# Two plain groups in place of one at the start of each Strassen mixer

## The chip, the cores and the metric

The kernel runs on one core of a Trainium2 chip (trn2). The metric is the device time of one execution in microseconds. Before the change the median of three runs is 1559.9 us (1555.95 to 1565.29). The engines are named as in the profile: PE is TensorE's matmul, PEld its weight load, DVE is VectorE, ACT ScalarE, POOL GpSimd, and SP the SyncE, whose queue issues nearly all DMAs.

## What is computed

Attention with RMS-normalised q and k, and then two mixers over its output. All of it is in float32, for 4 batches of 448 tokens with 768 channels.

```python
def _moe_ref(x, U, V, w_ch1, w_ch2):          # mixer a: w_ch1 is 768 x 3072, w_ch2 3072 x 768
    h = x.transpose(0, 2, 1) @ U @ V
    u = x + h.transpose(0, 2, 1)
    return u + np.maximum(u @ w_ch1, 0.0) @ w_ch2

def _moe2_ref(x, w_tok1, w_tok2, w_ch1, w_ch2):   # mixer b: w_ch1 is 768 x 1536, w_ch2 1536 x 768
    h = np.maximum(x.transpose(0, 2, 1) @ w_tok1, 0.0) @ w_tok2
    u = x + h.transpose(0, 2, 1)
    return u + np.maximum(u @ w_ch1, 0.0) @ w_ch2
...
x = attn_out.transpose(0, 2, 1, 3).reshape(4, 448, 768)
return _moe2_ref(_moe_ref(x))
```

## The kernel before

**Numbers.** Every matmul operand is a pair of float32r tiles, a high part (ScalarE copies and rounds it) and a low part (what is left, by VectorE or GpSimd). A product takes three matmuls for each block of 128 channels: high x high, low x high, high x low. The helper `mm` (L79) records every one, so all of TensorE's rows show line 79 and are told apart by tile: ps_g is a plain first layer, ps_p a Strassen product, ps_x the second layer, ps_u and ps_t the token mixing ahead of a mixer, ps_o a transpose of the output.

**Order of the work.** The four batches go in two pairs. Attention of all batches runs beside the first pair's mixers a and b (`ffn`). Then the second pair goes through mixer a and mixer b, both in `pair_ffn`; this is the Strassen part, from about 1006 us to the end. The program is written as one stream and a list scheduler fixes the order on each engine at build time; an engine works its own list strictly in order and waits on semaphores. DMAs of chunks, copies and stores all stand on SP's queue, in order too.

**A mixer in `pair_ffn`.** The hidden columns are cut into chunks of 128, and G = 2 chunks make a group: 24 chunks or 12 groups in mixer a, 12 chunks or 6 groups in mixer b. The first and the last group are plain: for each batch `plain` makes 18 matmuls a chunk (6 channel blocks x 3) into a PSUM bank, `relu` splits the result into gs, and `second` adds gs x w2 onto the batch's own tile (xs, the tile xT) in six steps of 6 matmuls, each ended by a VectorE add (L664). The groups between take both batches at once with Strassen's method (`seven`): the two batches are its two columns, the group's two chunks its two rows, and the channels are cut in halves. Seven products of 9 matmuls replace the plain first layer's 72.

**What the products read.** On the weights' side `w1_blocks` loads the group's two w1 chunks (tiles w_a, tag "raw", two buffers), builds the sums s1 to s4 on VectorE (L223 to L226) and splits seven blocks, the low parts on GpSimd (L145). On the activations' side the sums t1 to t4 of the two batches' u are needed; they are made once a mixer. Since `second` overwrites u in place, the sums must be taken from u before that. In the kernel before, `keep_first` (L571) copies the first batch's u by two DMAs (L576) into the low halves of t3 and t4 before its `second` runs, and `sums` (L580) reads the second batch's u in place, in three steps of four subtractions (L592 to L596) and four splits (L587 on ScalarE, L588 on VectorE). All twelve splits stand in program order ahead of the second batch's `second` and of the first Strassen group.

```python
        drain(second(xs[0], [plain(us[0], ws) for ws in w1s], w2s))
        g1 = [plain(us[1], ws) for ws in w1s]
        b = sums(kept)
        ...
        rest_ = second(xs[1], g1, w2s)
        for j0 in range(G, n - G, G):
            ...
            for _ in seven(a, b, gs):
                next(rest_, None)
                next(rest_, None)
```

`rest_` is the second layer that is still open; two of its steps are written after each product, and the scheduler mixes them. For the first Strassen group it is the second batch's six steps, for all later ones the twelve steps of the group before.

**Buffers.** The weight chunks w (high and low) have four buffers each, so two groups' chunks do not fit at once beside a group in use: a chunk's load, issued by SP straight into the low buffer, waits until the matmuls that read the buffer's last content are through. PSUM banks: three for kind "m", two each for "s" and "p". The pool act has two buffers of the tag xT; the second pair holds one of them, and t1 takes the other.

Of the kernel before, what the change touches and what calls it, by code (L numbers as in the profile page):

```python
# [10 lines left out]
F32R = mybir.dt.float32r  # L11
U32 = mybir.dt.uint32
I64 = mybir.dt.int64
AF = mybir.ActivationFunctionType
# [10 lines left out]
def attention_then_two_mixers(  # L25
# [49 lines left out]
    def f(x):  # L75
        return x.bitcast(F32)
# [132 lines left out]
    def tmp():  # L209
        return pools["pu"].tile([P, S], F32, tag="pu", name="pu")  # L210
# [354 lines left out]
    def pair_ffn(nm, w1, w2, xs, us, a, after, half=None, last=lambda: None):  # L565
# [5 lines left out]
        def keep_first():  # L571

            ts = [pools["tb"].tile([P, 2, HC, S], F32R, tag=f"t{i}", name=f"t{i}")
                  for i in (2, 3, 4)]
            for h, t in enumerate(ts[1:]):
                nc.sync.dma_start(f(t[:, 1]), xs[0][:, h * HC:(h + 1) * HC])  # L576
            return ts

        def sums(kept):


            ts = [act.tile([P, 2, HC, S], F32R, tag="xT", name="t1")] + kept
            k3, k4 = kept[1:]
            x = xs[1]

            def part(t, c, v_):
                nc.scalar.activation(t[:, 0, c], v_, AF.Copy)  # L587
                nc.vector.tensor_sub(t[:, 1, c], v_, f(t[:, 0, c]))  # L588

            for c in range(HC):  # L590
                t1, t2, t3 = [tmp() for _ in range(3)]
                nc.vector.tensor_sub(t1, x[:, c], f(k3[:, 1, c]))  # L592
                nc.vector.tensor_sub(t2, x[:, HC + c], t1)
                nc.vector.tensor_sub(t3, x[:, HC + c], x[:, c])
                t4 = tmp()
                nc.vector.tensor_sub(t4, f(k4[:, 1, c]), t2)  # L596
                for t, v_ in zip(ts, (t1, t2, t3, t4)):
                    part(t, c, v_)
            return {f"t{i + 1}": (t[:, 0], t[:, 1]) for i, t in enumerate(ts)}
# [80 lines left out]

        w1s, w2s = chunks(0)
        kept = keep_first()
        drain(second(xs[0], [plain(us[0], ws) for ws in w1s], w2s))
        g1 = [plain(us[1], ws) for ws in w1s]
        b = sums(kept)
        b.update(b11=(uh[:, :HC], ul[:, :HC]), b21=(uh[:, HC:], ul[:, HC:]),
                 b22=(vh[:, HC:], vl[:, HC:]))
        rest_ = second(xs[1], g1, w2s)
        for j0 in range(G, n - G, G):
# [128 lines left out]
    def last():  # L818
        pools["split_u"] = nc.vector
        blocks.append(w1_blocks("a", G))  # L820
# [7 lines left out]
    pair_ffn("a", wa1, wa2, xs, us, blocks[0], mix, last=lambda: blocks.append(w1_blocks("b", G)))  # L828
# [33 lines left out]
```

## Time and profile before

| | |
|---|---|
| median of three runs | 1559.9 us |
| the profiled execution | 1559.57 us, of it a span of 1556.9 us |
| mean granted clock of TensorE | 0.984 |
| busy in the span: PE, PEld | 1465.8 us (94%), 1295.5 us (83%) |
| busy in the span: DVE, POOL, ACT | 1101.6 (71%), 813.9 (52%), 708.8 us (46%) |
| ps_x matmuls | 2592 |
| ps_g matmuls | 1584 |

The profile lists instructions with line, engine, the tiles written and read, and the idle time of the engine ahead of them with what ended it. Matmuls overlap, so the busy time of a matmul (some 370 ns) is longer than the time from one start to the next; lost time on TensorE is read from starts.

### The profile page before, as it was taken

The page shows a single profiled execution, that of the slowest core. Times are in us where ns is not written, and L with a number is a line of the kernel's source. Part 1 is how long each engine was busy: PE and PEld are TensorE (multiplying, and loading weights), DVE is VectorE, ACT ScalarE, POOL GpSimd, SP SyncE. Part 2 cuts the span into 40 slices and gives each one's busy share as a digit, 9 for nine tenths or more (in the row PEclk, how much of TensorE's full clock was granted, in tenths as well). Part 3 has the DMA queues.
Part 4 walks back from the last instruction along what each step waited for, and adds up shares of the span by engine and source line. Part 5 has one row for each costly group of instructions (what it writes and reads, how often), then busy time and mean ns, then how long its engine had stood idle before and what let it go on. Part 6 is the DMA issues. An engine that isn't in the chain of part 4 may idle for free.

```text
span 1556.9 us, 21606 instructions
## 1 busy us (share of the span) xinstructions
PE 1465.8 (94%) x7522; PEld 1295.5 (83%) x7522; DVE 1101.6 (71%) x1800; ACT 708.8 (46%) x1413; POOL 813.9 (52%) x844
## 2 busy tenths in 40 slices
PE   4998878999999999999899999899999999999998
PEld 3766667788888999888798998789999999988997
DVE  5897777887888888566958676596666665576753
ACT  4776755566666665343634443342322322342311
POOL 6988867777786665444735553042443523113420
PEclk9999978999999999999999999999999999999999
DMA  6566553656655444442515530411212111101202
GB/s 171 143 158 168 143 177 108 189 164 187 189 175 151 142 149 134 165 154 81 180 49 187 184 132 28 156 61 52 71 52 71 44 50 60 66 21 51 72 21 92
DMA packets 96588, 180.94 MB, mean 116 GB/s; under 512 B 8992, under 2 KB 66304, under 8 KB 96480
## 3 DMA queue, kind: packets, MB, share of 16 engines
q1 hardware_dynamic: 96160, 179.57, 37.7%
q8 instruction: 59, 0.97, 0.3%
q14 instruction: 49, 0.40, 0.1%
q10 hardware_dynamic: 320, 0.00, 0.0%
HBM read 107.19 MB, written 36.57 MB: 92 GB/s over the span
## 4 chain that ended last, share of the span: by engine, by line
PE 65%; DVE 11%; DMA 7%; POOL 6%; ACT 5%; issue 4%; SPq 1%; ACTq 0%; POOLq 0%; DVEq 0%
PE ps_x L79 26%; PE ps_g L79 14%; PE ps_p L79 10%; PE pv L79 3%; PE sc L79 3%; PE pt L360 2%; POOL w_bits L134 2%; PE ps_u L79 2%; DMA c_a<-w_bits 2%; PE ps_t L79 2%; DVE w_bits L126 2%; POOL w L145 1%; DMA ks<-both 1%; DVE w_bits L131 1%; DMA qs<-both 1%
## 5 line engine op out<-in xcount | busy, mean ns | idle before, releaser
L79 PE MATMUL ps_x<-gs,w 128*128 128x448 f32 x2592 | 577.7, 371 | 14.7 <-DVE xT L664 4.2
L79 PEld LDWEIGHTS ps_x<-gs,w 128*128 128x128 f32 x2592 | 485.0, 190 | 60.1 <-DVE xT L534 7.8
L79 PE MATMUL ps_g<-u,w 128*128 128x448 f32 x1584 | 343.9, 370 | 0.5 <-POOL u L443 0.3
L79 PEld LDWEIGHTS ps_g<-u,w 128*128 128x128 f32 x1584 | 296.1, 189 | 25.3 <-POOL u L443 0.7
L145 POOL TENSOR_TENSOR w<-w 128x768 fp32r<-128x768 f32 x44 | 87.0, 1984 | 223.8 <-ACT w L144 142.4
L134 POOL TENSOR_TENSOR w_bits<-w_bits,w_round 128x768 uint32<-128x768 uint32 (+3 forms) x80 | 144.0, 1799 | 105.7 <-DVE w_bits L131 41.7
L145 POOL TENSOR_TENSOR w<-w_bits,w 128x768 fp32r<-128x768 f32 (+3 forms) x82 | 148.3, 1816 | 75.9 <-ACT w L144 72.2
L664 DVE TENSOR_TENSOR xT<-ps_x,xT 128x448 f32<-128x448 f32 x216 | 128.4, 618 | 63.5 <-PE ps_x L79 62.3
L534 DVE TENSOR_TENSOR xT<-ps_x,xT 128x448 f32<-128x448 f32 x216 | 132.4, 618 | 41.0 <-PE ps_x L79 38.2
L341 POOL TENSOR_SCALAR p<-p,sm 112x448 f32<-112x448 f32 x192 | 133.8, 709 | 19.9 <-DVE sm L338 17.2
L334 ACT ACTIVATE p<-sc,nm 112x448 f32<-112x448 f32 x192 | 121.1, 634 | 49.6 <-DVE nm L332 46.9
L79 PE MATMUL sc<-ks,qs 128*112 128x448 f32 x384 | 118.7, 402 | 18.8 <-ACT p L334 13.4
L145 POOL TENSOR_TENSOR w_a<-w_a 128x384 fp32r<-128x384 f32 (+1 forms) x28 | 42.9, 1533 | 178.7 <-DVE w_t L223 122.7
L332 DVE TENSOR_REDUCE nm<-sc 112x1 f32<-112x448 f32 x192 | 116.1, 615 | 19.9 <-PE sc L79 18.9
L360 PEld LDWEIGHTS pt<-ident,p 112*112 112x112 f32 x768 | 89.2, 133 | 36.4 <-issue 11.0
L360 PE MATMUL pt<-ident,p 112*112 112x112 f32 x768 | 111.5, 260 | 4.5 <-POOL p L341 3.4
L635 DVE TENSOR_TENSOR pu<-ps_p,pu 128x448 f32<-128x448 f32 x98 | 59.2, 620 | 71.0 <-PE ps_p L79 70.9
L126 DVE TENSOR_SCALAR w_bits<-w_bits 128x768 f32<-128x768 f32 (+3 forms) x80 | 75.5, 943 | 45.5 <-ACT w_bits L125 45.3
L371 ACT ACTIVATE ph<-pt 112x448 fp32r<-112x448 f32 (+1 forms) x168 | 88.2, 544 | 35.8 <-PE pt L360 35.1
L130 ACT ACTIVATE w_round<-w_raw 128x768 uint32<-128x768 uint32 (+3 forms) x80 | 69.7, 872 | 74.8 <-POOL w_bits L134 71.3
L375 DVE TENSOR_TENSOR pl<-pt,ph 112x448 fp32r<-112x448 f32 x144 | 87.3, 615 | 11.1 <-ACT ph L371 10.8
L125 ACT ACTIVATE w_bits<-w_raw 128x768 f32<-128x768 f32 (+3 forms) x80 | 69.9, 876 | 53.3 <-POOL w L145 36.5
(106 smaller groups left out, 2285.3 us busy)
## 6 DMA issues: line engine op xcount, KB each, us to landing
w_raw<-in_moe_w_ch_dram SPq DMA_DIRECT2D x72, 768.0 KB, 4.4
ks<-both SPq DMA_DIRECT2D x92, 224.0 KB, 3.7
c_a<-w_bits SPq DMA_DIRECT2D x48, 384.0 KB, 3.1
qs<-both SPq DMA_DIRECT2D x96, 112.0 KB, 3.1
w<-c_a SPq DMA_DIRECT2D x28, 384.0 KB, 3.7
c_b<-w_bits SPq DMA_DIRECT2D x24, 384.0 KB, 3.2
w_a<-c_a SPq DMA_DIRECT2D x20, 384.0 KB, 2.9
w<-c_b SPq DMA_DIRECT2D x16, 384.0 KB, 3.5
```

What stands on the lines that cost most here:

```text
L79: nc.tensor.matmul(o, lhsT=l, rhs=r, start=start, stop=stop)
L126: nc.vector.tensor_scalar_max(f(w), f(w), TINY)
L134: nc.gpsimd.tensor_tensor(w, w, r, op=ALU.add)
L145: nc.gpsimd.tensor_sub(lo, w, f(hi))
L332: nc.vector.tensor_reduce(nm, sc, axis=AX.X, op=ALU.max, negate=True)
L334: nc.scalar.activation(p, sc, AF.Exp, bias=nm, accum_out=sm[:, c % 2:c % 2 + 1])
L341: nc.gpsimd.tensor_scalar(x, x, sm[:, i:i + 1], 1.0, op0=ALU.mult, op1=ALU.mult)
L360: nc.tensor.transpose(pt[:, c * CP:(c + 1) * CP], pr[c][:, kc * CP:(kc + 1) * CP], ident[:CP, :CP],)
L371: nc.scalar.activation(ph, pt, AF.Copy)
L375: nc.vector.tensor_sub(pl, pt, f(ph))
L534: nc.vector.tensor_add(xT[:, dc], px, xT[:, dc])
L664: nc.vector.tensor_add(xT[:, dc], px, xT[:, dc])
```

## The change

Each mixer begins with two plain groups instead of one, so its Strassen loop starts a group later. Both batches' u are now kept by DMA copies (four a mixer, L577), the sums read the copies alone, and their twelve splits are a generator that is written step by step between the steps of two second layers. The second batch's part of the second plain group, first layer and second, becomes `rest_` of the first Strassen group. `w1_blocks` is called ahead of time for chunk 2G instead of G. The lines of `relu`, `plus` and `second` move up by seven (L664 becomes L657, L615 L608, L635 L628); L588 becomes L591.

```diff
-        def keep_first():
-
-            ts = [pools["tb"].tile([P, 2, HC, S], F32R, tag=f"t{i}", name=f"t{i}")
-                  for i in (2, 3, 4)]
-            for h, t in enumerate(ts[1:]):
-                nc.sync.dma_start(f(t[:, 1]), xs[0][:, h * HC:(h + 1) * HC])
+        def keep():
+
+            t1 = act.tile([P, 2, HC, S], F32R, tag="xT", name="t1")
+            ts = [t1] + [pools["tb"].tile([P, 2, HC, S], F32R, tag=f"t{i}", name=f"t{i}")
+                         for i in (2, 3, 4)]
+            for t, x, h in ((ts[2], 0, 0), (ts[3], 0, 1), (ts[1], 1, 0), (ts[0], 1, 1)):
+                nc.sync.dma_start(f(t[:, 1]), xs[x][:, h * HC:(h + 1) * HC])
             return ts
 
-        def sums(kept):
...
+        def sums(ts):
 
             for c in range(HC):
...
-                nc.vector.tensor_sub(t1, x[:, c], f(k3[:, 1, c]))
-                nc.vector.tensor_sub(t2, x[:, HC + c], t1)
-                nc.vector.tensor_sub(t3, x[:, HC + c], x[:, c])
-                t4 = tmp()
-                nc.vector.tensor_sub(t4, f(k4[:, 1, c]), t2)
+                y2, x2, x1, y1 = [f(t[:, 1, c]) for t in ts]
+                t1, t2, t3, t4 = [tmp() for _ in range(4)]
+                nc.vector.tensor_sub(t1, x2, x1)
+                nc.vector.tensor_sub(t2, y2, t1)
+                nc.vector.tensor_sub(t3, y2, x2)
+                nc.vector.tensor_sub(t4, y1, t2)
                 for t, v_ in zip(ts, (t1, t2, t3, t4)):
-                    part(t, c, v_)
+                    nc.scalar.activation(t[:, 0, c], v_, AF.Copy)
+                    nc.vector.tensor_sub(t[:, 1, c], v_, f(t[:, 0, c]))
+                    yield
...
-        w1s, w2s = chunks(0)
-        kept = keep_first()
-        drain(second(xs[0], [plain(us[0], ws) for ws in w1s], w2s))
-        g1 = [plain(us[1], ws) for ws in w1s]
-        b = sums(kept)
+        def plains(i, ws):
+            return second(xs[i], [plain(us[i], w) for w in ws[0]], ws[1])
+
+        ws = chunks(0)
+        ts = keep()
+        parts = sums(ts)
+        drain(plains(0, ws))
+        for _ in plains(1, ws):
+            next(parts)
+        ws = chunks(G)
+        for _ in plains(0, ws):
+            next(parts)
+        drain(parts)
+        b = {f"t{i + 1}": (t[:, 0], t[:, 1]) for i, t in enumerate(ts)}
...
-        rest_ = second(xs[1], g1, w2s)
-        for j0 in range(G, n - G, G):
+        rest_ = plains(1, ws)
+        for j0 in range(2 * G, n - G, G):
...
-        blocks.append(w1_blocks("a", G))
+        blocks.append(w1_blocks("a", 2 * G))
...
-    pair_ffn("a", wa1, wa2, xs, us, blocks[0], mix, last=lambda: blocks.append(w1_blocks("b", G)))
+    pair_ffn("a", wa1, wa2, xs, us, blocks[0], mix, last=lambda: blocks.append(w1_blocks("b", 2 * G)))
```

The scheduler's order changes from the first product with t2 on; ahead of that all engines' lists are the same but for the copies. Three places of it matter.

TensorE at the start of mixer a, in the changed program. Here t_11118 is t2 and t_11119 is t3, and w_s and w_a are the weight blocks of the first Strassen group. The 17 and 19 ps_g are the first layer of the first plain group for the second batch, the 18 and 18 that of the second plain group for the first batch.

```order
L79 MATMUL ps_p<-u,w_a 128x448 x9
L79 MATMUL ps_g<-u,w 128x448 x17
L79 MATMUL ps_x<-gs,w 128x448 x6
L79 MATMUL ps_g<-u,w 128x448 x19
L79 MATMUL ps_x<-gs,w 128x448 x30
L79 MATMUL ps_p<-t_11118,w_s 128x448 x5
L79 MATMUL ps_g<-u,w 128x448 x18
L79 MATMUL ps_x<-gs,w 128x448 x6
L79 MATMUL ps_g<-u,w 128x448 x18
L79 MATMUL ps_p<-t_11118,w_s 128x448
L79 MATMUL ps_x<-gs,w 128x448 x3
```

Before, the first two matmuls with t2 came 4 ps_x after the 19 ps_g. Now they come 30 later, and five of them stand ahead of the second plain group. In mixer b the order between the last ps_u and the first two matmuls with t2 is 4 ps_g, 9 ps_p and 14 ps_g.

TensorE at the change from the first to the second Strassen group of mixer a. First before: t_11119 is t4, the product whose end frees the tile w_a for the next group; u,w_s is the product with s4; the next group begins with u,w_a, and t_11117,w_s is its first matmul with t2.

```order
L79 MATMUL ps_p<-t_11119,w_a 128x448
L79 MATMUL ps_x<-gs,w 128x448 x2
L79 MATMUL ps_p<-u,w_s 128x448 x9
L79 MATMUL ps_x<-gs,w 128x448 x3
L79 MATMUL ps_p<-u,w_a 128x448 x2
L79 MATMUL ps_x<-gs,w 128x448 x15
L79 MATMUL ps_p<-t_11117,w_s 128x448
L79 MATMUL ps_x<-gs,w 128x448 x6
```

And the same place in the changed program, where t_11117 is t1, t_11120 is t4 and t_11118 is t2:

```order
L79 MATMUL ps_x<-gs,w 128x448 x24
L79 MATMUL ps_p<-u,w_s 128x448 x9
L79 MATMUL ps_p<-t_11117,w_s 128x448 x3
L79 MATMUL ps_x<-gs,w 128x448 x6
L79 MATMUL ps_p<-t_11117,w_s 128x448 x6
L79 MATMUL ps_p<-t_11120,w_a 128x448 x9
L79 MATMUL ps_x<-gs,w 128x448 x9
L79 MATMUL ps_p<-u,w_a 128x448 x2
L79 MATMUL ps_x<-gs,w 128x448 x15
L79 MATMUL ps_p<-t_11118,w_s 128x448
L79 MATMUL ps_x<-gs,w 128x448 x12
```

The product with s4 (u,w_s) has moved from behind the product with t4 to ahead of it. From the end of the t4 product to the ps_x that follows the first matmul with t2 there are 2 + 9 + 3 + 2 + 15 + 1 = 32 matmuls before, and 9 + 2 + 15 + 1 = 27 now. The same place in mixer b has 36 before and 27 now. The six ps_x in the middle of the t1 product are the last to read the second plain group's w2 chunks; 15 matmuls lie between them and the end of the t4 product.

VectorE at that place in mixer a, in the changed program. L628 is the addition of two products, L608 the low half of a relu, L223 to L226 form the next group's s1, s3, s2 and s4, and L657 adds a second layer's step onto xT and so frees its PSUM bank.

```order
L628 TENSOR_TENSOR pu<-ps_p,pu 128x448 x5
L608 SCALAR_TENSOR_TENSOR gs<-pu,gs 128x448 x3
L223 TENSOR_TENSOR w_t<-w_a 128x384
L224 TENSOR_TENSOR w_t<-w_a 128x384
L225 TENSOR_TENSOR w_t<-w_t,w_a 128x384
L226 TENSOR_TENSOR w_t<-w_a,w_t 128x384
L657 TENSOR_TENSOR xT<-ps_x,xT 128x448 x7
```

Before, two of the relu halves (L615 there) came ahead of L223 and the third between L225 and L226; now all three come ahead.

## Rows read from the trace of the kernel before

**Rows 1.** The page, part 1: busy time, share of the span, instructions.

```profile
PE 1465.8 (94%) x7522; PEld 1295.5 (83%) x7522; DVE 1101.6 (71%) x1800; ACT 708.8 (46%) x1413; POOL 813.9 (52%) x844
```

**Rows 2.** TensorE's timeline: start, length (us), instruction, count.

```profile
1086.69 2.59 PE L79 MATMUL ps_x<-gs,w 128*128 128x448 f32 x12
...
1089.12 1.99 PE L79 MATMUL ps_p<-t,w_a 128*128 128x448 f32 x9
```

**Rows 3.** TensorE's timeline, a later change of Strassen groups.

```profile
1075.67 0.44 PE L79 MATMUL ps_p<-t,w_s 128*128 128x448 f32 x1 [0.37 <-DVE xT L664]
```

**Rows 4.** Stretches: length, PE, PEld, DVE, ACT, POOL (count), PEclk, DMA, GB/s.

```profile
1024.91:1027.11 2.20, 0.99 (x4) 0.50 (x4) 2.20 (x5) 1.91 (x5) 0.00 (x0) 1.00 0.00 0
1036.12:1045.25 9.13, 6.92 (x33) 5.83 (x31) 8.92 (x11) 4.19 (x8) 6.98 (x6) 1.00 0.13 44
1392.96:1398.47 5.51, 4.46 (x18) 2.96 (x17) 5.51 (x12) 4.03 (x8) 1.52 (x1) 1.00 0.41 143
1411.24:1422.38 11.14, 7.72 (x37) 6.58 (x35) 9.72 (x11) 5.11 (x9) 8.86 (x6) 1.00 0.21 70
1422.38:1426.90 4.52, 4.51 (x15) 4.06 (x15) 2.17 (x4) 0.03 (x1) 3.02 (x3) 0.62 0.01 4
```

**Rows 5.** TensorE's timeline; in brackets idle time and its end.

```profile
1026.60 0.68 PE L79 MATMUL ps_p<-t,w_s 128*128 128x448 f32 x2 [1.21 <-ACT t L587]
...
1394.83 1.49 PE L79 MATMUL ps_x<-gs,w 128*128 128x448 f32 x6 [0.43 <-ACT gs L614]
...
1045.25 1.48 PE L79 MATMUL ps_x<-gs,w 128*128 128x448 f32 x6 [2.12 <-DVE xT L664]
...
1422.38 2.58 PE L79 MATMUL ps_x<-gs,w 128*128 128x448 f32 x6 [2.12 <-DVE xT L664]
```

**Rows 6.** Instructions on tile ps_p: count, shortest, median, longest (ns).

```profile
L79 PE MATMUL ps_p<-u,w_s x126: 362/365/370, 1036.5 to 1500.8; 128*128 128x448 f32 x126
```

**Rows 7.** Groups by line and shape, from 1006 us: count, busy us, mean ns, idle.

```profile
L664 DVE TENSOR_TENSOR xT<-ps_x,xT 128x448 f32<-128x448 f32 x216 | 128.4, 618 | 63.5 <-PE ps_x L79 62.3
```

**Rows 8.** Landing times of the copies, those of mixer a, then of mixer b.

```profile
DMA to landing us min/median/max: 6.0/7.0/8.1
...
DMA to landing us min/median/max: 3.3/3.7/4.1
```

**Rows 9.** Groups by line and shape from 1006 us, ScalarE.

```profile
L587 ACT ACTIVATE t<-pu 128x448 fp32r<-128x448 f32 x24 | 13.4, 575 | 14.5 <-DVE pu L592 7.2 <-DVE pu L596 4.1 <-DVE pu L593 1.9
```

**Rows 10.** TensorE's timeline, last ps_u ahead of mixer b.

```profile
1386.07 1.38 PE L79 MATMUL ps_u<-w,xs 128*128 128x448 f32 x6
```

**Rows 11.** SP's timeline: issues of w and w_a loads at the change of groups.

```profile
1030.68 0.93 SPq L194 DMA_DIRECT2D w<-c_a  x2
...
1036.32 0.32 SPq L217 DMA_DIRECT2D w_a<-c_a  x1
...
1408.84 0.93 SPq L194 DMA_DIRECT2D w<-c_b  x2
...
1411.47 0.32 SPq L217 DMA_DIRECT2D w_a<-c_b  x1
```

**Rows 12.** The page, part 6: DMA issues, size, median us to landing.

```profile
w<-c_a SPq DMA_DIRECT2D x28, 384.0 KB, 3.7
...
w_a<-c_a SPq DMA_DIRECT2D x20, 384.0 KB, 2.9
```

**Rows 13.** GpSimd's timeline in mixer b, the two w splits.

```profile
1412.97 4.04 POOL L145 TENSOR_TENSOR w<-w 128x768 fp32r<-128x768 f32 x2 [10.58 <-ACT w L144]
```

**Rows 14.** VectorE's timeline at the change of groups, mixer b.

```profile
1415.76 1.67 DVE L223 TENSOR_TENSOR w_t<-w_a 128x384 f32<-128x384 f32 x1
...
1417.82 1.36 DVE L225 TENSOR_TENSOR w_t<-w_t,w_a 128x384 f32<-128x384 f32 x1
...
1419.11 1.42 DVE L615 SCALAR_TENSOR_TENSOR gs<-pu,gs 128x448 fp32r<-128x448 f32 x1
...
1420.45 1.35 DVE L226 TENSOR_TENSOR w_t<-w_a,w_t 128x384 f32<-128x384 f32 x1
```

More of the change, by code (lines that the diff above doesn't have):

```diff
@@ L569, in pair_ffn @@
         (uh, ul), (vh, vl) = us
-        def keep_first():
-            ts = [pools["tb"].tile([P, 2, HC, S], F32R, tag=f"t{i}", name=f"t{i}")
-                  for i in (2, 3, 4)]
-            for h, t in enumerate(ts[1:]):
-                nc.sync.dma_start(f(t[:, 1]), xs[0][:, h * HC:(h + 1) * HC])
-            return ts
-        def sums(kept):
[L582 to L588, printed above, removed]
-            for c in range(HC):
-                t1, t2, t3 = [tmp() for _ in range(3)]
-                nc.vector.tensor_sub(t1, x[:, c], f(k3[:, 1, c]))
-                nc.vector.tensor_sub(t2, x[:, HC + c], t1)
-                nc.vector.tensor_sub(t3, x[:, HC + c], x[:, c])
-                t4 = tmp()
-                nc.vector.tensor_sub(t4, f(k4[:, 1, c]), t2)
+        def keep():
[4 more added lines that the diff above has]
+                nc.sync.dma_start(f(t[:, 1]), xs[x][:, h * HC:(h + 1) * HC])
+            return ts
+        def sums(ts):
+            for c in range(HC):
+                y2, x2, x1, y1 = [f(t[:, 1, c]) for t in ts]
[4 more added lines that the diff above has]
+                nc.vector.tensor_sub(t4, y1, t2)
                 for t, v_ in zip(ts, (t1, t2, t3, t4)):
-                    part(t, c, v_)
-            return {f"t{i + 1}": (t[:, 0], t[:, 1]) for i, t in enumerate(ts)}
+                    nc.scalar.activation(t[:, 0, c], v_, AF.Copy)
+                    nc.vector.tensor_sub(t[:, 1, c], v_, f(t[:, 0, c]))
+                    yield
         def plain(u, ws):
```

## The prediction, made before the changed kernel was run

> **What bounds the kernel now.** I read the page first, then TensorE's timeline, then equal stretches of it, and last the queues and engines that feed the places where it stands. The page shows TensorE busy in 94% of the span [rows 1]. That is a busy share and no rate, so I took the rate from a stretch without a wait: twelve matmuls of 448 columns that start at 1086.69 are followed by the next group at 1089.12 [rows 2]. That is 2.43 / 12 = 0.2025 us each, and this is the price of a matmul below. In the Strassen part (1006 us to the end) TensorE starts its matmuls at about this spacing nearly everywhere: the later groups lose 0.4 us or less in one place [rows 3]. So there the time is the number of matmuls times 0.2025, plus the few stretches in which TensorE stands. What other engines save costs or gains nothing unless it shortens such a stretch.
>
> **Where it stands.** Five stretches, all at the start of a mixer, hold nearly all of it [rows 4]. The counts there include one matmul that still runs at the left edge, so I take one off each (for the first, 4 less 1 gives 3). Length less count times 0.2025:
> - mixer a, first product with t2: 2.20 - 3 x 0.2025 = 1.59 us
> - mixer a, change from the first Strassen group to the second: 9.13 - 32 x 0.2025 = 2.65
> - mixer b, first product with t2: 5.51 - 17 x 0.2025 = 2.07
> - mixer b, the same change of groups: 11.14 - 36 x 0.2025 = 3.85
> - mixer b, right after it: 4.52 - 14 x 0.2025 = 1.68, and here the granted clock is 0.62, so much of it ran at the lower of the two levels (1.2 instead of 2.4 GHz), after the engine had stood twice within 3 us.
>
> The sum is 11.84 us. What ended these waits [rows 5]: the sums that make t2 (L587, and the relu that queues with them), and at the change of groups a VectorE add, L664, which frees the PSUM bank that the next ps_x needs. That add was not itself slow; it stood in VectorE's queue behind L223 to L226, the four operations that form the next group's weight blocks.
>
> **The change, part by part.**
>
> *Matmuls.* The row of the product with s4 counts 126, nine a product, so there are 14 Strassen groups [rows 6]. Two become plain. A Strassen group has 7 x 9 = 63 matmuls ahead of its second layer, a plain one 2 x 2 x 18 = 72; the second layer is the same. That is 2 x 9 = 18 matmuls more, 18 x 0.2025 = +3.65 us, all on the path.
>
> *Work that leaves the other engines.* 24 VectorE, 13 ScalarE and 8 GpSimd instructions fewer. TensorE's pace hides them wherever it doesn't stand, so I cost them at nothing; were that cover gone, VectorE's 24 at 0.618 us [rows 7] would be worth 15 us at the most.
>
> *The copies and the sums.* Two more copies a mixer (the halves of the second batch's u), on SP's queue ahead of the last stores and of all chunk loads of the second plain group. In mixer a the last one waits for the old xT tile's last transposes. From these TensorE has 9 + 17 + 6 + 19 = 51 matmuls (10.3 us) to the end of the first plain group's relus, where the sums come up, and the two copies made there today took 6.0 and 8.1 us [rows 8]; that fits. The sums have more matmuls to hide behind than today, but the new order puts five matmuls of s2 x t2 ahead of the second plain group on TensorE, which need two of the three column blocks of t2. After that relu stand, one behind the other, the relu's two halves, six VectorE operations and ScalarE's half of t2: 0.58 + 7 x 0.62 + 0.58 = 5.5 us [rows 7, 9], and up to 2 us more if a GpSimd split falls beside them. TensorE comes there after 33 matmuls, 6.7 us. I bound the loss by 0 and 1.6 (today's), and take 0.9. In mixer b the last ps_u matmuls start at 1386.07 [rows 10] and end at 1387.3. From there the chain is a VectorE add (0.62), the issue (0.46 [rows 11]), the copy (3.3 to 4.1, as in mixer b today [rows 8]), the sum (0.62) and ScalarE's half of t2 (0.58): 1392.9 to 1393.7. TensorE arrives after 4 + 9 + 14 = 27 matmuls, at 1392.8. That loses 0.1 to 0.9, and t2's lower half and the relus queued behind it some 0.7 more; I take 1.4 (bounds 0 and, with a landing of 8.1, 5.6). Together 2.3 where today 3.66 is lost: -1.4 us.
>
> *Chunks of the second plain group.* Their w slots come free only as the first plain group ends. The w1 loads then have 53 matmuls (10.7 us), the w2 loads, behind the last ps_x, 33 (6.7 us). A load takes 3.7 us to land [rows 12], ScalarE's half about 1.0 (0.58 for 448 columns, so an estimate for 768) and GpSimd's 2.0 [rows 13]: 6.7. So this is just met, and I cost it at nothing; half a microsecond a mixer would show first.
>
> *The change of groups.* This I expect to get longer. Its length is a chain: the fourth t product ends and frees the raw tile, SP issues the next w_a load, it lands 2.9 us later [rows 12], ScalarE, VectorE (L223 to L226) and GpSimd split it, and only then L664 frees the bank. From the end of that product to the ps_x it takes 9.13 us in mixer a and 11.14 in mixer b [rows 4]. The difference is when the two w loads ahead of it leave: 5.4 us before the product's end in mixer a (1030.68 against 1036.12), 2.4 in mixer b (1408.84 against 1411.24) [rows 11]. In mixer b their GpSimd halves run from 1412.97 for 4.04 us [rows 13], and VectorE's L223 takes 1.67 us, L615 1.42 and L226 1.35 [rows 14], where the same engine's L664 takes 0.62. In the changed program the two loads wait for slots that the second layer of the second plain group frees, 15 matmuls or 3.0 us before the end of the fourth product, in both mixers: nearly mixer b's case. On the other side the L615 that sat between L225 and L226 is gone from there (three such operations now come ahead of L223). I take 10.1 us, between the two, and 9.13 and 11.14 as bounds. And TensorE has less to do meanwhile: from the fourth product to the ps_x that needs the bank the new order has 9 + 2 + 15 + 1 = 27 matmuls, 5.47 us, in place of 32 and 36, because the product with s4 now comes before it. So it loses 10.1 - 5.47 = 4.6 us in each mixer, 9.3 in place of 6.5: +2.8 us.
>
> A rule of the Trainium skill bears on this. The rows show two-input VectorE operations on SBUF at twice their length while GpSimd is at work [rows 13, 14], while L664, with one input in PSUM, keeps its 0.62 [rows 7]. The skill (SBUF — State Buffer, section "Who interferes with whom") says that a VectorE instruction with two SBUF inputs and a GpSimd instruction that reads SBUF exclude each other, the first to issue keeping the port for its whole length. The trace agrees for L223 to L226; by that rule seven such operations in a row (three relu halves, four block sums) would stand behind GpSimd here, which is the second rival below.
>
> *Clock.* One spell at the lower level today (1.68 us). With waits of 4.6 us I expect one again, perhaps two; bounds 0 and 3.36. I take 1.68: no difference.
>
> *Sum.* +3.65 - 1.4 + 2.8 + 0 = +5.05, on the profiled execution's 1559.57 us: 1564.6 us. (That execution stands 0.3 us under the median of the three runs, 1559.9, which lie within 9.3 us.) About 0.5%, 7.8 us, is what a measurement can tell from no change, so this counts as no change.
>
> **The rivals.**
> 1. *The waits go.* Two plain groups give the loads and sums enough time, and the chain at the change of groups shrinks to its bare parts (2.9 landing, four block sums at 0.55, one add 0.62, about 6.2 us), so each mixer loses 0.7 there, nothing at t2, and no clock spell. 3.65 - 11.84 + 1.4 = -6.8: 1552.8 us. For it speaks that later groups lose next to nothing [rows 3]; against it that the new order takes five to nine matmuls out of the cover. Even all five stretches gone gives 8.2 us, hardly more than what can be told. Chance 0.17, a third of it faster by over 0.5%.
> 2. *GpSimd shuts VectorE out (the other side).* At the change of groups all seven two-input operations meet the w splits, the chain is mixer b's 11.14 or longer, both mixers lose 5.7 us or more, t2 in mixer a keeps its 1.6, and both get a spell at the lower clock: 3.65 + (1.6 + 1.4 - 3.66) + (11.4 - 6.5) + 1.68 = +9.6: 1569.2 us. It decides from a chain of about 10.8 us on. For it speaks mixer b's row; against it that the three relu halves could run before GpSimd starts. Chance 0.18.
> 3. *The copy of the second batch's u is late.* In mixer b it lands after 8.1 us, as the longest did in mixer a, instead of 3.3 to 4.1: 5.6 us lost at t2 in place of 1.4, so 1568.8 us. For it speaks that copies which leave together took twice as long [rows 8]; against it that in mixer b little else is moving then. Chance 0.08.
> 4. *The change does little of either:* the five stretches keep their length and only the matmuls count, 1563.2 us; this lies in the forecast's own range.
>
> **How the numbers follow.** The forecast (with case 4) has 0.57, rival 1 0.17, rival 2 0.18, rival 3 0.08. Faster by over 0.5%: a third of rival 1 and a little for a bound that I missed, 0.07. Slower by over 0.5%: nearly all of rival 2, most of rival 3 and a tenth of the forecast, 0.17 + 0.06 + 0.04 = 0.27. Within: 0.66. The range goes from 1555.5, short of rival 1, to 1572, past rival 2 with a late copy of 2 us.
>
> **What would show it.** In the changed profile: ps_g rows 144 more and ps_p rows 126 fewer, and 0.2025 us between matmuls as before. Up to 1017 us the two timelines should agree. At the change from first to second Strassen group, a wait of 4 to 5 us in each mixer that ends at the add into xT, with L223 to L226 above 1 us each and GpSimd at work beside them. If the four take 0.55 each, the first rival is right; if they and the relu halves all stretch, the second. At t2 a wait under 2 us in each mixer; one of 5 in mixer b that ends at a copy is the third. The prediction is wrong if a wait of over 3 us stands anywhere else, at the chunks of the second plain group above all.

## The result, and the profile after

The changed kernel took 1569.6 us (median of 17 runs, 1564.7 to 1576.2); the kernel before, run beside it, 1559.9 us (17 runs, 1555.5 to 1565.3). The ratio is **1.0055, with a 95% interval of 1.0041 to 1.0069**: slower by 8.6 us (6.4 to 10.8), where +4.7 was forecast against the same median. The two medians themselves lie 9.7 us apart; the ratio is used below. The time lies inside the range, at the value of the second rival (1569.2 us), and just past the half per cent that counted as no change.

First the page of the changed kernel, part 1, which answers to [rows 1], and a row of the view by tile (count, then shortest, median and longest in ns).

```profile
PE 1474.5 (94%) x7540; PEld 1296.5 (83%) x7540; DVE 1089.7 (70%) x1778; ACT 703.5 (45%) x1403; POOL 808.1 (52%) x836
```

```profile
L79 PE MATMUL ps_p<-u,w_s x108: 362/368/369, 1058.8 to 1510.3; 128*128 128x448 f32 x108
```

TensorE has 18 matmuls more (7540 against 7522), and the product with s4 went from 126 to 108 [rows 6]: two groups fewer, as counted. Next the stretches in which TensorE stands, cut at its matmul starts as in [rows 4]: length, then busy time and count of PE, PEld, DVE, ACT and POOL, granted clock, DMA share, GB/s. They are, for mixer a and then for mixer b: the first product with t2, the second plain group's chunks, the change from the first Strassen group to the second, and what follows it.

```profile
1021.30:1023.68 2.38, 1.06 (x4) 0.38 (x2) 2.38 (x5) 0.58 (x1) 0.17 (x1) 1.00 0.00 0
1032.76:1033.81 1.05, 0.37 (x2) 0.00 (x0) 0.41 (x1) 0.89 (x2) 0.00 (x0) 1.00 0.03 12
1067.76:1075.20 7.44, 4.13 (x17) 2.67 (x15) 7.40 (x9) 3.40 (x7) 5.29 (x5) 0.93 0.02 8
1075.20:1081.16 5.96, 5.95 (x16) 5.31 (x17) 2.79 (x5) 0.00 (x0) 4.00 (x4) 0.52 0.00 0
1401.03:1403.07 2.04, 1.97 (x8) 1.24 (x7) 2.04 (x5) 1.88 (x4) 0.00 (x0) 1.00 0.80 315
1407.73:1409.06 1.33, 0.77 (x4) 0.38 (x2) 1.33 (x3) 0.00 (x0) 1.33 (x2) 1.00 0.00 0
1451.32:1458.69 7.37, 3.94 (x17) 2.74 (x15) 7.34 (x9) 3.04 (x7) 5.75 (x5) 1.00 0.02 8
1458.69:1464.03 5.34, 5.33 (x18) 4.80 (x19) 2.79 (x5) 0.00 (x0) 4.01 (x4) 0.68 0.00 0
```

Each count holds one matmul that still runs over the left edge, except in the fourth and eighth row, ahead of which TensorE stood. Length less starts times 0.2025 us:

| lost, us | before | forecast | after |
|---|---|---|---|
| t2, mixers a + b | 1.59 + 2.07 | 2.3 | 1.77 + 0.62 = 2.39 |
| chunks of the second plain group | - | 0 | 0.85 + 0.72 = 1.57 |
| change of groups | 2.65 + 3.85 | 9.3 | 4.20 + 4.13 = 8.33 |
| lower clock after it | 0 + 1.68 | 1.68 | 2.72 + 1.69 = 4.41 |
| sum | 11.84 | 13.3 | 16.70 |

16.70 - 11.84 + 3.65 for 18 matmuls = +8.5 us, close to the 8.6 of the ratio. The two profiled executions differ by more: from the first start of a ps_p to the last of a ps_x it is 543.2 us before (1006.66 to 1549.89) and 554.4 after (1004.47 to 1558.87), 11.2 us. The 2.7 us that the table doesn't hold are matmuls that follow one another a little more slowly in some stretches, without a wait (last section).

Now the change of groups in mixer a, from the timeline (start, length, engine, line, operation, count; in brackets idle time and what ended it).

```profile
1063.71 1.99 PE L79 MATMUL ps_p<-t,w_a 128*128 128x448 f32 x9
...
1065.53 1.99 PE L79 MATMUL ps_x<-gs,w 128*128 128x448 f32 x9
1065.72 0.32 SPq L217 DMA_DIRECT2D w_a<-c_a  x1
1065.94 3.66 POOL L145 TENSOR_TENSOR w<-w 128x768 fp32r<-128x768 f32 x2 [9.04 <-ACT w L144]
...
1067.77 3.38 DVE L608 SCALAR_TENSOR_TENSOR gs<-pu,gs 128x448 fp32r<-128x448 f32 x3 [0.88 <-ACT gs L607]
1068.65 0.53 ACT L144 ACTIVATE w_a<-w_a 128x384 fp32r<-128x384 f32 x1
...
1070.67 1.09 PE L79 MATMUL ps_x<-gs,w 128*128 128x448 f32 x4 [0.49 <-DVE gs L608]
1071.07 0.55 DVE L223 TENSOR_TENSOR w_t<-w_a 128x384 f32<-128x384 f32 x1
...
1071.75 1.19 POOL L145 TENSOR_TENSOR w_a<-w_a 128x384 fp32r<-128x384 f32 x1 [2.15 <-DVE w_t L223]
1072.01 1.34 DVE L225 TENSOR_TENSOR w_t<-w_t,w_a 128x384 f32<-128x384 f32 x1
...
1073.38 1.23 DVE L226 TENSOR_TENSOR w_t<-w_a,w_t 128x384 f32<-128x384 f32 x1
1073.96 0.63 PE L79 MATMUL ps_p<-t,w_s 128*128 128x448 f32 x1 [2.21 <-ACT w_s L144]
...
1074.54 2.20 DVE L657 TENSOR_TENSOR xT<-ps_x,xT 128x448 f32<-128x448 f32 x4
...
1075.21 4.10 PE L79 MATMUL ps_x<-gs,w 128*128 128x448 f32 x10 [0.62 <-DVE xT L657]
```

The w_a load leaves as the fourth t product ends (1065.70) and has landed by 1068.65, when ScalarE reads it. But L223, which needs it, starts 2.4 us later: VectorE was still at three relu halves (L608), which took 3.38 us. Then L225 and L226 alternate with GpSimd's w_a splits, and L657, which frees the bank, comes last (L664 is L657 in the changed program). TensorE stands three times: for a relu half (0.49 us idle), for a weight block (2.21) and for the add that frees the bank (0.62). From the first matmul behind the fourth t product (1065.53) to the ps_x that needs the bank (1075.21) it is 9.7 us here and 9.6 in mixer b; 10.1 was forecast between the same two points.

### The profile page after: what moved, and what is told of

It reads as the page before. It is cut to its first block, busy times and chain, and to the rows that moved or that the text cites. A ratio compares the mean times of both kernels' runs of the same rounds, so it can differ in the third digit from the quotient of the medians.

```text
span 1566.2 us, 21601 instructions
## 1 busy us (share of the span) xinstructions
PE 1474.5 (94%) x7540; PEld 1296.5 (83%) x7540; DVE 1089.7 (70%) x1778; ACT 703.5 (45%) x1403; POOL 808.1 (52%) x836
## 4 chain that ended last, share of the span: by engine, by line
PE 69%; DVE 9%; POOL 7%; DMA 6%; issue 4%; ACT 4%; SPq 1%; DVEq 0%; POOLq 0%; ACTq 0%
PE ps_x L79 27%; PE ps_g L79 17%; PE ps_p L79 9%; PE pv L79 4%; PE sc L79 4%; PE pt L360 3%; POOL w_bits L134 2%; POOL w L145 2%; PE ps_u L79 2%; DVE w_bits L126 2%; DMA qs<-both 2%; PE ps_t L79 2%; DVE w_bits L131 1%; POOL p L341 1%; DVE w_bits L127 1%
## 5 line engine op out<-in xcount | busy, mean ns | idle before, releaser
L79 PE MATMUL ps_g<-u,w 128*128 128x448 f32 x1728 | 375.6, 370 | 1.1 <-POOL w L145 0.6
L79 PEld LDWEIGHTS ps_g<-u,w 128*128 128x128 f32 x1728 | 323.9, 189 | 28.7 <-POOL u L443 0.9
L145 POOL TENSOR_TENSOR w<-w 128x768 fp32r<-128x768 f32 x48 | 95.8, 2004 | 261.2 <-ACT w L144 177.2
L657 DVE TENSOR_TENSOR xT<-ps_x,xT 128x448 f32<-128x448 f32 x216 | 127.3, 617 | 81.9 <-PE ps_x L79 80.4
L145 POOL TENSOR_TENSOR w_a<-w_a 128x384 fp32r<-128x384 f32 (+1 forms) x24 | 37.0, 1541 | 155.6 <-DVE w_t L223 111.3
L628 DVE TENSOR_TENSOR pu<-ps_p,pu 128x448 f32<-128x448 f32 x84 | 50.2, 620 | 64.6 <-PE ps_p L79 64.4
```

Of the source, the lines that this page charges most:

```text
L79: nc.tensor.matmul(o, lhsT=l, rhs=r, start=start, stop=stop)
L145: nc.gpsimd.tensor_sub(lo, w, f(hi))
L657: nc.vector.tensor_add(xT[:, dc], px, xT[:, dc])
```

## The experiments

Ratios are to the kernel before, run on the same chip, with 95% intervals; 0.1% is 1.56 us. An edit shifts the lines behind it: the relu's low half (L608 in the changed kernel, L615 before) is L611 in e3 and e5 and L610 in e9, the add into xT (L657, L664) is L660, L659 and, in e12, L666, and the first block sum (L223) is L226 in e3 and e5.

**e1, the second plain group alone.** Two copies and all sums as before, then a second plain group:

```diff
-        rest_ = second(xs[1], g1, w2s)
-        for j0 in range(G, n - G, G):
+        drain(second(xs[1], g1, w2s))
+        w1s, w2s = chunks(G)
+        drain(second(xs[0], [plain(us[0], ws) for ws in w1s], w2s))
+        rest_ = second(xs[1], [plain(us[1], ws) for ws in w1s], w2s)
+        for j0 in range(2 * G, n - G, G):
```

> The second plain group alone: two copies, all sums made in the first plain group as before. Theory A (the cost is 18 matmuls, 3.65 us, and a longer wait at the change of Strassen groups, whose cover of 27 matmuls comes with the second plain group): that wait is 4 us or more in each mixer as in the changed kernel, so 1568 us (1565 to 1572). Theory B (the copies of the second batch's u and the spread sums are what costs): only the matmuls are added, 1563.6 us (1561 to 1566), and the change of groups waits 2.1 us as before.

1566.8 us, ratio 1.0040 (1.0025 to 1.0056): +6.2 us. The ratio alone lies between the two theories; the trace decides for theory A. The waits at the change of groups are there without the new copies. In mixer a 15 matmuls start from 1067.32 to 1074.68, so 7.36 - 3.04 = 4.3 us is lost there:

```profile
1070.60 1.09 PE L79 MATMUL ps_x<-gs,w 128*128 128x448 f32 x4 [0.89 <-DVE gs L615]
...
1074.68 1.65 PE L79 MATMUL ps_x<-gs,w 128*128 128x448 f32 x6 [2.99 <-DVE xT L664]
```

**e2, the four copies alone.** `keep` and `sums` of the change, with the one plain group of the kernel before; `drain(sums(ts))` stands where `sums(kept)` stood.

> The four copies alone: one plain group as before, the sums made there from the copies. Theory A: within 1.5 us of the kernel before, 1558.5 to 1562, with the change of groups as before (2 to 4 us) and a wait for a copy of 1 us at most. Theory B: the late copies cost 4 us or more, 1564 us and above, with a wait at t2 that ends at a copy.

1564.6 us, ratio 1.0026 (1.0010 to 1.0041): +4 us, the size that theory B gave, though its mechanism, a late copy, shows in mixer b alone. In mixer a TensorE waits for the sums that follow one another on VectorE and ScalarE; in mixer b VectorE stands 4.08 us until a copy has landed, and TensorE stands behind it at t2 (the first of these rows is of mixer a, the other two of mixer b):

```profile
1028.31 1.11 PE L79 MATMUL ps_p<-t,w_s 128*128 128x448 f32 x2 [1.42 <-ACT t L590]
...
1394.93 0.62 DVE L586 TENSOR_TENSOR pu<-t,pu 128x448 f32<-128x448 f32 x1 [4.08 <-DMA t<-xT]
...
1396.22 0.68 PE L79 MATMUL ps_p<-t,w_s 128*128 128x448 f32 x2 [1.84 <-ACT t L590]
```

With the second plain group the same copies are covered: in mixer b of the changed kernel VectorE still stands 2.12 us for one, but TensorE has other matmuls, and t2 loses 0.62 us.

```profile
1398.67 0.62 DVE L586 TENSOR_TENSOR pu<-t,pu 128x448 f32<-128x448 f32 x1 [2.12 <-DMA t<-xT]
```

So four copies need the second group. Whether the two parts simply add can't be told from the times: e1 and e2 cost 6.2 and 4 us, both together 8.6, each with some 2 us either way.

**e3, GpSimd's part left out, at the wrong place.** For the chunks of one group in each mixer the subtraction goes:

```diff
+        if low:
             split(f(lo), hi, lo)
+        else:
+            nc.scalar.activation(hi, f(lo), AF.Copy)
...
-            w2s = [w2_chunk(nm, w2, j0 + i) for i in range(G)]
+            w2s = [again(f"{nm}2_{j0 + i}", j0 != 2 * G) for i in range(G)]
```

> The changed kernel with its two GpSimd subtractions for the w2 chunks of the first Strassen group left out in each mixer (the low half then holds the whole weight, so those products are not the reference's). Theory A2 (GpSimd draws out the three relu halves on VectorE, and these hold the chain at the change of groups): the three take 0.62 us each instead of 1.13 to 1.23, the chain is 1.5 to 1.8 us shorter in each mixer, 1566.3 us (1563 to 1567.5). Theory C (the w_a load that waits for the fourth t product holds the chain): L223 starts at the same distance from that product and the time stays at 1569.6 us (1568 to 1571).

1569.1 us, ratio 1.0040 (1.0022 to 1.0058). It does not bear on the question: the splits beside the relu halves are still there. They belong to the chunks of the second Strassen group. What went had run 11 and 16 us earlier in mixer a (at 1055.04 and 1049.98 in the changed kernel); the 28.00 in the row is the idle time of GpSimd that is left, and the expectation of e5 takes it for the distance.

```profile
1067.40 3.67 POOL L145 TENSOR_TENSOR w<-w 128x768 fp32r<-128x768 f32 x2 [28.00 <-ACT w L144]
...
1069.26 3.37 DVE L611 SCALAR_TENSOR_TENSOR gs<-pu,gs 128x448 fp32r<-128x448 f32 x3 [0.85 <-ACT gs L610]
```

**e5, the same for the right chunks** (`j0 != 3 * G`).

> The changed kernel with two GpSimd subtractions left out in each mixer, now those for the w2 chunks of the second Strassen group, which run beside the three relu halves (e3 left out those of the first, which ran some 28 us earlier). The low half then holds the whole weight, so those products are not the reference's. Theory A2 (GpSimd draws out the relu halves, and these hold the chain at the change of groups): the three take 0.62 us each instead of 1.13 to 1.23, L223 starts 1.5 us earlier after the fourth t product, and the time is 3 us shorter than that of the changed kernel: 1.0035 times the kernel before (1.0025 to 1.0045) instead of 1.0055. Theory C (the landing of w_a holds the chain): L223 starts where it did, 5.4 us after the end of that product, and the ratio stays at 1.0055.

Ratio 1.0004 (0.9983 to 1.0025), where the changed kernel has 1.0055: 8 us less, and theory A2. The relu halves and what follows, in mixer a:

```profile
1063.74 0.32 SPq L220 DMA_DIRECT2D w_a<-c_a  x1
...
1065.55 1.70 DVE L611 SCALAR_TENSOR_TENSOR gs<-pu,gs 128x448 fp32r<-128x448 f32 x3 [0.65 <-ACT gs L610]
...
1067.16 0.55 DVE L226 TENSOR_TENSOR w_t<-w_a 128x384 f32<-128x384 f32 x1
...
1071.33 4.25 PE L79 MATMUL ps_x<-gs,w 128*128 128x448 f32 x12 [0.79 <-DVE xT L660]
```

The three take 1.70 us, and the first block sum starts 3.4 us after the w_a issue, not 5.4. From 1065.77, where the last 15 ps_x ahead of the waits begin, to 1071.33 there are 16 starts: 5.56 - 3.24 = 2.3 us lost in place of 4.2; mixer b loses 2.5. The lower clock lasts 8 matmuls in mixer a (1.4 us, not 2.7) and does not come in b. That is 6.5 us of the 8; I had expected 3, since I left the clock out. TensorE, VectorE and ScalarE work the same lists as in the changed kernel.

**e9, nothing left out, only GpSimd's queue re-ordered:** the two subtractions go behind the last block split of the second Strassen group.

```diff
-            w2s = [w2_chunk(nm, w2, j0 + i) for i in range(G)]
+            with tc.issue_after(last_low[0].ins) if j0 == 3 * G else ExitStack():
+                w2s = [w2_chunk(nm, w2, j0 + i) for i in range(G)]
```

> The changed kernel with nothing left out: the two GpSimd subtractions that e5 dropped are queued on GpSimd behind the last block split of the second Strassen group. Theory A2 (three relu halves drawn out by these two): they take 0.62 us each, the wait at the change of groups falls from 4.1 to about 2.3 us a mixer and the lower clock after it is short or gone, as in e5: 1.0015 times the kernel before (0.9995 to 1.003). Theory D (e5 gained because GpSimd had less to do in all): 1.004 to 1.0055, as the changed kernel.

1562.6 us, ratio 1.0004 (0.9987 to 1.0021): theory A2, and theory D falls, for GpSimd does as much as before, and the lists of TensorE, VectorE and ScalarE are those of the changed kernel:

```profile
1065.31 1.70 DVE L610 SCALAR_TENSOR_TENSOR gs<-pu,gs 128x448 fp32r<-128x448 f32 x3 [0.47 <-ACT gs L609]
...
1071.09 4.17 PE L79 MATMUL ps_x<-gs,w 128*128 128x448 f32 x12 [0.78 <-DVE xT L659]
...
1075.04 3.65 POOL L145 TENSOR_TENSOR w<-w 128x768 fp32r<-128x768 f32 x2
```

**e12, the edit of e9 on the kernel before** (`j0 == 2 * G`, its second Strassen group).

> The edit of e9 on the kernel before: the two GpSimd subtractions for the w2 chunks of its second Strassen group behind the last block split of that group. Theory A2: in mixer a nothing, since there L223 waited for w_a and not for the relu halves; in mixer b one relu half (1.91 us) and L223 (1.67 us) take 0.6 each, -2 us, and the 1.7 us at the lower clock may go with them: 0.9985 times the kernel before (0.997 to 0.9995), which is less than the half per cent that e9 took off the changed kernel. Rival: the same half per cent comes off here, 0.995, and the collision is then no part of what the change costs.

1557.1 us, ratio 0.9957 (0.9938 to 0.9976): outside A2's range, and close to the rival's number. The trace shows mixer a as expected and mixer b better:

```profile
1046.44 1.49 PE L79 MATMUL ps_x<-gs,w 128*128 128x448 f32 x6 [2.13 <-DVE xT L666]
```

```profile
1418.79 0.37 PE L79 MATMUL ps_x<-gs,w 128*128 128x448 f32 x1
...
1424.11 1.88 PE L79 MATMUL ps_p<-t,w_s 128*128 128x448 f32 x8 [0.89 <-POOL w_s L145]
```

In mixer a the wait at L664's place stays (2.12 in [rows 5], 2.13 here). In mixer b 21 matmuls start from 1418.79 to 1424.11, so 5.32 - 4.25 = 1.1 us is lost there in place of 3.85 + 1.68: 4.5 us less, which the interval (3.7 to 9.7) holds. The relu half of 1.91 us and the block sum of 1.67 us take 0.63 and 0.56 there. But TensorE's list changed a little as well: eight products with t2 (the second row) now come ahead of the six ps_x that waited for the add in [rows 5], and how much of the 4.5 us is due to that is not separated. So the collision of GpSimd's splits with VectorE cost the kernel before too, in one mixer; after the change it costs in both. The edit takes 0.0051 off the changed kernel and 0.0043 off the kernel before, and with it in both the changed kernel is still slower by 1.0004 - 0.9957 = 0.0047, or 7 us (some 4 us either way): most of what the change adds is not the collision.

**e4 and e6, second-layer adds ahead of the block sums.** In the changed kernel (e4) and in the one before (e6, with `2 * G`) the four block sums of the second Strassen group are queued behind four adds into xT:

```diff
+            if j0 == 3 * G:
+                for _ in range(4):
+                    add = next(rest_)
+                with tc.issue_after(add.ins):
+                    a = w1_blocks(nm, j0)
             a = a or w1_blocks(nm, j0)
```

(`second` hands out its add for this with `yield add`.) The edit draws four steps of the second layer, 24 ps_x with their adds, ahead in the program, so TensorE's list changes together with VectorE's: 18 and then 30 ps_x stand ahead of the first product with t2 (the first two rows below), where 15 stood.

> The changed kernel with the four block sums of the second Strassen group queued on VectorE behind four adds into xT. Theory A3 (the waits at the change of groups exist because the bank-freeing adds stand behind the block sums on VectorE): the waits of 2.2 and 1.2 us there go and 0.8 us for the relu halves stays, -3.4 us in each mixer, and the two spells at the lower clock that follow (2.7 and 1.7 us) go too: 1558.4 us (1556 to 1562). Theory C (the weights of the second group are late whatever the order on VectorE): the same wait comes up at the first product that needs a block sum, and 1567 to 1570 us remain. If the spells stay although the waits go: 1563 us.

> The kernel before with the four block sums of its second Strassen group queued on VectorE behind four adds into xT, as e4 did to the changed kernel. Theory A3: the waits at the change of groups (2.65 and 3.85 us) and the spell of 1.68 us go, some 1.2 us a mixer come up at the next change as in e4: -5.8 us, 0.9963 times the kernel before (0.995 to 0.998). The rest of the change (18 matmuls at 3.65, the late chunks 1.75, less 1.0 gained at t2) then stands between e4 and this one: e4 is slower by 4 us. Theory C: no difference from the kernel before, 0.9995 to 1.001.

e4: 1557.1 us, ratio 0.9972 (0.9955 to 0.9990). e6: 1555.5 us, ratio 0.9945 (0.9924 to 0.9966). Both are faster than either kernel, e6 by more than A3's range, and the waits at the change of groups go as A3 said. That VectorE's order alone does it is not shown, since TensorE's moved with it. Of e4 (the first two rows mixer a's change of groups, the other two the next change):

```profile
1068.28 3.88 PE L79 MATMUL ps_x<-gs,w 128*128 128x448 f32 x18
...
1072.58 6.35 PE L79 MATMUL ps_x<-gs,w 128*128 128x448 f32 x30
...
1095.79 3.20 PE L79 MATMUL ps_x<-gs,w 128*128 128x448 f32 x15
...
1099.98 0.47 PE L79 MATMUL ps_p<-t,w_s 128*128 128x448 f32 x1 [0.99 <-ACT w_s L144]
```

From 1068.28 to 1072.58 there are 19 starts: 4.30 - 3.85 = 0.45 us lost where 4.2 was, though the relu halves still collide (3.70 us for three). No lower clock follows, in either mixer. Part of the wait comes up one change later: from 1095.79 to 1100.49, 16 starts, 1.46 us. e4 against e6 is +0.0027, or 4 us, as expected for the matmuls and chunks that remain; with some 4 us either way, this doesn't exclude no difference.

**e8 and e10, adds first in more groups of the kernel before:** in every later Strassen group (e8, `if not a:`), or in its second and third (e10).

> As e6, but the block sums of every later Strassen group stand behind four adds. Theory A3: the wait that moved to the next change goes as well, and the 0.3 us at some of the later changes: 0.994 times the kernel before (0.9925 to 0.9955). Rival: put off in every group, the block sums reach their products late, and each of 12 changes in a mixer waits 0.5 us or more for a block: 1.000 or above.

> As e6, with the block sums of the third Strassen group queued behind four adds as well. Theory A3: the waits that e6 shows at the change from the second to the third group (1.4 us in mixer a, 1.5 in b) become the 0.3 us that e8 shows there: -2.2 us against e6's 0.9945, so 0.993 times the kernel before (0.9915 to 0.9945). Rival: the wait moves on to the next change again, and the ratio stays at 0.9945 (0.994 to 0.996).

e8: 0.9961 (0.9946 to 0.9976). e10: 0.9970 (0.9957 to 0.9984). Neither improves on e6, and both miss A3's range. In e8 the order itself loses some 0.4 us at most changes of mixer a, as e4 does at the first. In e10 the rival's mechanism came, though the ratio lies above its 0.994 to 0.996: the wait moved on by another group, in mixer b as two stands, and eight matmuls at the lower clock follow:

```profile
1473.92 0.47 PE L79 MATMUL ps_p<-t,w_s 128*128 128x448 f32 x1 [1.54 <-ACT w_s L144]
1475.49 2.37 PE L79 MATMUL ps_p<-t,w_s 128*128 128x448 f32 x8 [1.10 <-POOL w_s L145]
```

**e11, e6 and e12 together.**

> Both edits on the kernel before: block sums of the second Strassen group behind four adds (e6), and the two GpSimd subtractions beside them queued behind its last block split (e9). Theory A: with the adds ahead nothing on TensorE's path waits for the relu halves and block sums there, so this is e6 again, 0.9945 (0.993 to 0.996). Rival: VectorE and GpSimd still hold each other up where the wait moved (the next change), and 2 us more go: 0.993 or below.

The ratio is 0.9962 (0.9941 to 0.9982), as e6 within what is measured: with the adds ahead, the later low halves gain nothing that shows. e6, e11 and e12 can't be ranked.

**e7, the price of a matmul.** The kernel before, with three products of a later group computed twice:

```diff
+                for rr in range(2 if again_ and l in ("s1", "s2", "s3") else 1):
...
+            for _ in seven(a, b, gs, j0 in (8 * G, 10 * G)):
```

> The kernel before with three products (s1, s2 and s3) of two later Strassen groups computed twice in each mixer, 108 matmuls more and nothing else: the price of a matmul that no wait surrounds. Theory A: 108 x 0.2025 = 21.9 us, 1.0140 times the kernel before (1.0130 to 1.0150). A rival: the other engines need the time, so that waits shrink and a matmul is worth less: 1.012 or below.

Mixer b has only four Strassen groups and reaches neither of the two, so 54 matmuls were added and not 108:

```profile
PE 1479.9 (94%) x7576; PEld 1303.6 (83%) x7576; DVE 1111.5 (71%) x1800; ACT 709.3 (45%) x1413; POOL 813.0 (52%) x844
```

Ratio 1.0059 (1.0038 to 1.0080): 9.2 us, or 0.17 each (0.11 to 0.23). 54 x 0.2025 = 10.9 us lies inside, so 18 matmuls at 3.65 us stand, though the interval is too wide to exclude 2 us.

## Why the prediction was right and where it was wrong

- **The model held, and that it comes so close is in part luck.** Matmuls times 0.2025 plus the stretches in which TensorE stands gives +8.5 us beside the measured 8.6 (6.4 to 10.8). But two things in it change from one execution to the next: the spells at the lower clock (below) and the spacing of matmuls, which makes the profiled executions differ by 2.7 us more than the sum.
- **Work that leaves the other engines, costed at nothing.** It is 22 VectorE, 10 ScalarE and 8 GpSimd instructions by the pages, not 24, 13 and 8; no term of the sum depends on it.
- **18 matmuls, +3.65:** as counted (7540 against 7522); the price agrees with e7.
- **t2, 2.3 us forecast:** 2.39 measured, but split the other way. Mixer a lost 1.77 where I took 0.9, mixer b 0.62 where I took 1.4: mixer b's late copy was covered, and mixer a waited for sums on VectorE and ScalarE.
- **Chunks of the second plain group, costed at nothing: wrong, 1.57 us.** I gave the w2 loads 33 matmuls of cover. The last ps_x that frees their slots starts at 1027.90 in mixer a; behind it come 18 ps_g and one ps_p, and then the ps_x that needs the new chunk:

```profile
1029.11 3.81 PE L79 MATMUL ps_g<-u,w 128*128 128x448 f32 x18
1032.76 0.37 PE L79 MATMUL ps_p<-t,w_s 128*128 128x448 f32 x1
1033.82 0.86 PE L79 MATMUL ps_x<-gs,w 128*128 128x448 f32 x3 [0.69 <-ACT w L144]
```

  That is 19 matmuls, 3.85 us, for an issue at 1028.54, the landing and ScalarE's half. The sentence on half a microsecond a mixer named the right place with too small a size.
- **Change of groups, 9.3 us forecast:** 8.33 measured, so the length was nearly right and the chain behind it was not. I let it begin with the w_a load. In fact w_a had landed 2.4 us before L223, and VectorE was held at a relu half. The wait that I forecast at the add alone came as three, the longest of them at a weight block. The cover of 27 matmuls was right: 9.7 - 27 x 0.2025 = 4.2.
- **The clock, costed at no difference: the largest miss, +2.7 us in these two executions.** 4.41 us was lost to the lower level in place of 1.68, past my upper bound of 3.36. I gave one spell; both mixers have one, at 0.52 and 0.68 granted. How much of the 2.7 us belongs to the change stays open. In e7, where all engines work the lists of the kernel before but for 54 matmuls in later groups of mixer a, both mixers have a spell too, and 1.67 + 2.56 = 4.23 us is lost to them; with that in place of 1.68, the sum above gives +6.0 and not +8.5. What makes the spell go is shown: in e4 and e6, where the waits at the change of groups go, none follows it, in e5 and e9 mixer b's goes.
- **The rivals.** The second has the right time, for its mechanism with other sizes: both mixers stand at the change, both have a spell. But the stand is 4.2 us and not 5.7, and the chain 9.7 and not 10.8 or more; chunks and a larger clock term make up for it, so its right time is luck. Of the seven operations that it had GpSimd draw out, one relu half (2.31 us) and two block sums were; L223 kept 0.55. The first and the third did not come: no wait of 5 us at a copy, and the block sums L225 and L226 were drawn out to 1.34 and 1.23 us.
- **The chances.** With 0.66 on no change and 0.27 on slower, the less likely side came, by a little: 0.41 to 0.69% against the bound of 0.5%. I had bounded the clock by the one spell that I had seen, although I forecast longer waits in both mixers.

## What to carry to other kernels

When a wait on the busiest engine ends at an operation of another, look at what holds that operation, in its own engine's queue and on other engines, and move work that is needed only 30 us later behind it: two GpSimd subtractions in each mixer, queued later, were worth 8 us here. Price a pause of TensorE with the lower clock that may follow it: in the profiled execution 4.4 us on 8.3 us of waits. A group of work that is put in to hide loads brings loads of its own, whose cover has to be counted in the order of instructions, from the one that frees the slot.

## What the runs showed of the hardware

**VectorE waits for GpSimd's operation to end.** The view of L608 at the change of groups in the changed kernel, mixer a (count, then shortest, median and longest in ns):

```profile
L608 DVE SCALAR_TENSOR_TENSOR gs<-pu,gs x3: 611/612/2307, 1067.8 to 1070.5; 128x448 fp32r<-128x448 f32 x3
```

It isn't a slowing of all three: one takes 2.31 us, the others 0.61; in e9 the three together take 1.70 us. The long one starts at 1067.77 and ends 0.47 us after GpSimd's two splits (1065.94 + 3.66 = 1069.60). The Trainium skill (SBUF — State Buffer, section "Who interferes with whom") says that a VectorE operation with two inputs in SBUF contends with a GpSimd operation that reads SBUF, and that the lock on the ports they share is exclusive; these rows agree, and e5 and e9, in which only GpSimd's part was taken away or moved, show it as the cause.

**The lower clock and the waits ahead of it.** The change of groups in e9, of mixer a and then of mixer b:

```profile
1069.84 0.47 PE L79 MATMUL ps_p<-t,w_s 128*128 128x448 f32 x1 [0.83 <-ACT w_s L144]
```

```profile
1450.79 0.47 PE L79 MATMUL ps_p<-t,w_s 128*128 128x448 f32 x1 [1.22 <-ACT w_s L144]
1452.04 2.74 PE L79 MATMUL ps_x<-gs,w 128*128 128x448 f32 x12 [0.79 <-DVE xT L659]
```

Mixer a stands 0.83 and 0.78 us, and the twelve ps_x after it take 4.17 us, much of it at the lower level; mixer b stands longer, 1.22 and 0.79, and its twelve take 2.74. So the length of these stands alone doesn't decide. Two executions with the same order show it too, the kernel before and e7 behind the first change of groups of mixer a (columns as in [rows 4]):

```profile
1045.25:1049.75 4.50, 4.50 (x22) 4.19 (x23) 2.29 (x5) 0.03 (x1) 3.06 (x3) 1.00 0.00 0
```

```profile
1042.83:1047.33 4.50, 4.50 (x14) 4.03 (x15) 2.16 (x4) 0.03 (x1) 3.02 (x3) 0.62 0.00 0
```

TensorE had stood idle 2.12 us ahead of the first and 2.13 us ahead of the second; one runs 22 matmuls at 1.00 granted, the other 14 at 0.62. What else decides is open.

**Two spacings at the full clock.** One stretch of the kernel before and, below it, of the changed kernel:

```profile
1100.00:1175.00 75.00, 74.83 (x370) 69.11 (x369) 46.63 (x72) 18.18 (x32) 29.83 (x22) 1.00 0.16 49
```

```profile
1100.00:1175.00 75.00, 75.00 (x365) 68.11 (x364) 46.08 (x72) 20.76 (x37) 33.41 (x24) 1.00 0.17 54
```

At 1.00 granted, where hardly anything waits, the changed kernel starts 365 matmuls in the time of 370. Nine of ps_p from 1117.75 to 1119.61 are 0.2067 us apart; nine in the kernel before, from 1112.23 to 1114.05, 0.2022. Every profiled execution here has such stretches of some 25 to 150 us, each at other places, that of the kernel before from about 1480 us on. No edit here governs them, their cause is open, and so single executions differ by a few microseconds for no reason in the kernel. The upstream part differs as well: the profiled execution of the changed kernel reaches mixer a 2.2 us earlier, ahead of anything that was changed.
